# Block transposes on VectorE and SBUF-to-SBUF DMA in place of TensorE transposes, in a fused attention and feed-forward kernel

## The chip, the cores and the metric

The kernel runs on one core of one Trainium2 chip. A core has five engines with a queue each: TensorE (PE in the profile, with its weight loads as PEld), VectorE (DVE), ScalarE (ACT), GpSimd (POOL) and SyncE (SP, which here only issues DMA transfers), and 16 DMA engines that they share. The metric is the device time of one execution in microseconds; lower is better.

## The reference, cut to what matters

```python
xn = layernorm(x)                                  # x: 1 x 2048 x 640
qkv = xn @ wqkv                                    # 640 x 1920; 32 heads of 20
# position s attends to s, s-2, ..., s-14 (8 positions, 2 apart)
idx = pos[:, None] - 2 * arange(8)[None, :]
logits = einsum("bhsd,bhswd->bhsw", q, k[idx]) * 20 ** -0.5   # masked where idx < 0
o = einsum("bhsw,bhswd->bhsd", softmax(logits), v[idx])
s = o @ wo                                         # 640 x 640
g = silu(silu(xn @ w1) @ w2)                       # 640 x 1536, 1536 x 640
out = x + s * g
```

All inputs and the output are float32.

## The kernel before, in words

The 2048 positions are cut into four groups of 512: two halves of the sequence times even and odd positions, since the window of 8 steps by 2. In a group, a partition holds four positions (T = 4 tiles of 128), and attention works across the free dimension on VectorE.

Matrix products want the contracted dimension (640 = DC = 5 chunks of 128) on the partitions, so both the normalised x (`XIN`) and the attention output (`O`) must be turned from position-major to feature-major. TensorE reads fp32 data in a reduced form, so each operand is split into a high half (ScalarE's copy) and a low half (VectorE's difference), and each product is three matmuls: hi x hi, lo x hi, hi x lo. `TH` and `TL` hold the turned halves, two buffers each: one for the group's x, the other alternately for the previous group's turned o and the next group's turned x.

- `split_t` turns one chunk: four PE transposes into a `ROT` bank of PSUM (L429), ScalarE's high half (L433), VectorE's low half (L434).
- `qkv_phase(g)`: four quarters of eight heads (`CQ` = 160 columns); five weight chunks each, all four tiles (L633 to L635). ScalarE moves results to `KV` and `Q`; `halo` copies the neighbours' keys and values between partitions by DMA (L454); `scores` (L477, L480) and `values` (L509, L514, L517) are VectorE's attention. Between weight chunks, at the places in `O_AT`, `o_chunk` turns a chunk of the previous group's o.
- `wo_phase(g - 1)`: the previous group's output projection (L667, L669), its product with the gate `G` on VectorE (L699), the addition of x on POOL in `XR` (L706), and the store.
- `ffn_phase(g)`: twelve steps of w1 (L784 to L786), SiLU in two copies on ScalarE (L790, L791), the low half on VectorE (L792), w2 (L667, L669), and the gate's SiLU into `G` (L823). It loads and normalises the next group's x (L407, L419), and from step `XT_AT` = 7 on turns it a chunk per step. The last group turns its own o here, at `OL_AT`, and `wo_last` ends the kernel.
- The first group's x is turned by `first_quarter` (L558).

Weights come from DRAM once as float32 (`raw_load`, on SP), are split by ScalarE (L371) and VectorE or POOL (L374) into a slot of a ring of seven (`WR`), and are stored split to DRAM (L380, on SP); later uses fetch the split form through POOL's queue (L363). The ring runs seven weights ahead of PE.

The order on each engine is set before the kernel is built: `Weave.add` records every operation with the keys that it reads and writes, an estimated duration and a priority, and `Weave.order` plays them through a model of the engines (with `LANES` = 8 transfers in flight for a queue, `RATE` and `LAND` for a transfer). PE keeps the order of the program. Every other queue is emitted in the order of that model, so an instruction that has to wait on the chip holds back everything behind it in its queue. `lock` marks operations that the model keeps apart on VectorE and POOL.

Of the kernel before, what the change touches and what calls it, by code (L numbers as in the profile page):

```python
# [8 lines left out]
F32 = mybir.dt.float32  # L9
F32R = mybir.dt.float32r  # L10
AF = mybir.ActivationFunctionType
OP = mybir.AluOpType
# [19 lines left out]
WARM, WARM2 = 22, 3  # L32
HOLD = 3.4
LO = 10
X_AT = 2, 7, 8
TILE_AT = 1, 1.5, 5, 6
LOW_AT = 3
# [14 lines left out]


class Op:
    __slots__ = ("eng", "dur", "fn", "prio", "lock", "table", "nbytes", "seq", "left", "users", "ready", "start", "end")


class Weave:
# [16 lines left out]
        self.ops = []  # L75
        self.writer, self.readers = {}, {}

    def add(self, eng, dur, fn, reads=(), writes=(), prio=0.0, lock=False, table=None, nbytes=0):
        o = Op()
        o.eng, o.dur, o.fn, o.prio, o.lock, o.table, o.nbytes = eng, dur, fn, prio, lock, table, nbytes  # L80
# [12 lines left out]
        for k in reads:  # L93
            self.readers.setdefault(k, []).append(o)
        before.discard(o)
        o.left = len(before)
        for b in before:
            b.users.append(o)
        self.ops.append(o)
        return o  # L100

    def order(self):
# [12 lines left out]
        while len(done) < len(self.ops):  # L115
# [56 lines left out]
def local_attention_silu_ffn(ctx: ExitStack, tc: tile.TileContext, x, wqkv, wo, w1, w2, out):  # L172
# [19 lines left out]
    def tiles(name, n, shape, dtype=F32):  # L192
        return [sb.tile(shape, dtype, name=f"{name}{i}") for i in range(n)]
# [8 lines left out]
    SH = [None, sb.tile([P, TOK], F32R, name="sh1")]  # L202
    SL = [None, sb.tile([P, TOK], F32R, name="sl1")]
    ST.append(sb.tile([P, 2, 6], F32, name="st1"))
    SH[0] = sb.tile([P, TOK], F32R, name="sh0")
    SL[0] = sb.tile([P, TOK], F32R, name="sl0")
    SD = sb.tile([P, 2, T], F32, name="sd")
    mask = sb.tile([P, T, W], F32, name="mask")
    M = tiles("m", 2, [P, T, HQ])
# [44 lines left out]
        add("PE", dur, fn, reads, writes)  # L254
        clock[0] += dur

    def dma(fn, reads, writes, nbytes, prio, dur=0.45):
        add("SP", dur, fn, reads, writes, prio, nbytes=nbytes)

    clock = [0.0]  # L260

# [52 lines left out]
    def raw_load(k):  # L314
# [17 lines left out]
        if u[0] == "q":  # L332
            _, q, c = u
            w = qcols(q)
            all3 = wqkv[c * P:(c + 1) * P, :].rearrange("p (s m) -> p s m", s=3)

            def go():
                nc.sync.dma_start(r[:, :w], all3[:, 0, q * BQ:q * BQ + w])
                nc.sync.dma_start(r[:, w:].rearrange("p (s m) -> p s m", s=2), all3[:, 1:, q * CQ:(q + 1) * CQ])
            dma(go, [], kr, n * P * 4, 1 + k if k < 2 * DC else clock[0] + 5, dur=0.9)  # L340
            return
        elif u[0] == "w1":
            src = w1.rearrange("(c p) f -> p c f", p=P)[:, :, u[1] * P:(u[1] + 1) * P]
            dst = r.rearrange("p (c f) -> p c f", c=DC)
        else:
            m = wo if u[0] == "wo" else w2
            src, dst = m[u[1] * P:(u[1] + 1) * P, :], r
        dma(lambda: nc.sync.dma_start(dst, src), [], kr, n * P * 4, 1 + k if k < 2 * DC else clock[0] + 5)

    def w_load():  # L350
# [8 lines left out]
        kh, kl = ("wh", s), ("wl", s)  # L359
        due = clock[0]  # L360
        if what[i] == "load":
            src = halves[u]
            add("POOL", 1.0, lambda: nc.gpsimd.dma_start(both, src), [("half", u)], [kh, kl], due + 10,  # L363
                nbytes=2 * n * P * 4)
            return
# [57 lines left out]
    def split_t(src, skeys, c, i):  # L423
# [3 lines left out]
        def turn():  # L427
# [6 lines left out]
        dve(TOK, lambda: nc.vector.tensor_tensor(out=lo, in0=ps, in1=hi.bitcast(F32), op=OP.subtract),  # L434
            [kp] + kh, kl, 0)


    def evac_qkv(g, q, t, ps, kp):
        kv, w = KV[q], qcols(q)
# [81 lines left out]
    def o_chunk(g, c, i):  # L521
        qs = range(c * P // CQ, ((c + 1) * P - 1) // CQ + 1)
        split_t(O, [("o", q, t) for q in qs for t in (0, 2)], c, i)
# [92 lines left out]
        return ps  # L616

    def qkv_phase(g, i, io):
        for q in range(NQ):
            if g == 0 and q == 0:  # L620
                ps = first_quarter(i)
            else:
                ps = [bank() for t in range(T)]
                for c in range(DC):
# [10 lines left out]
                            nc.tensor.matmul(o, hi, wl, start=False, stop=c == DC - 1)  # L635
# [18 lines left out]
    O_AT = {(1, 1): 0, (1, 4): 1, (2, 3): 2, (3, 1): 3, (3, 3): 4}  # L654
    OL_AT = {8: 0, 9: 1, 10: 2, 11: 3, 12: 4}
    XT_AT = 7

    def tm_banks():
        a = [bank() for t in range(T)]
# [207 lines left out]
```

## Time and profile before

| | |
|---|---|
| runs shown, median (lowest to highest) | 642.38 us (642.08 to 643.38), 3 runs |
| the profiled execution's own time | 642.85 us |
| its span in the trace | 641.1 us |
| TensorE, VectorE, ScalarE, POOL busy | 634.1, 538.5, 207.3, 116.7 us |
| moved by DMA | 162.44 MB, mean 253 GB/s |
| TensorE transposes of x and o past the first x (L429) | 140 |

Busy time of an engine is the time in which at least one of its instructions runs; for PE, whose matmuls overlap, it says little on its own. In rows of a group, the numbers behind the bar are busy us and the mean ns of one, then the idle time before them and what ended it. In rows of the timeline and the chain, the first number is the start in us and the second the duration in us.

### The profile page before, as it was taken

The page shows a single profiled execution, that of the slowest core. Times are in us where ns is not written, and L with a number is a line of the kernel's source. Part 1 is how long each engine was busy: PE and PEld are TensorE (multiplying, and loading weights), DVE is VectorE, ACT ScalarE, POOL GpSimd, SP SyncE. Part 2 cuts the span into 40 slices and gives each one's busy share as a digit, 9 for nine tenths or more (in the row PEclk, how much of TensorE's full clock was granted, in tenths as well). Part 3 has the DMA queues.
Part 4 walks back from the last instruction along what each step waited for, and adds up shares of the span by engine and source line. Part 5 has one row for each costly group of instructions (what it writes and reads, how often), then busy time and mean ns, then how long its engine had stood idle before and what let it go on. Part 6 is the DMA issues. An engine that isn't in the chain of part 4 may idle for free.

```text
span 641.1 us, 9080 instructions
## 1 busy us (share of the span) xinstructions
PE 634.1 (99%) x3497; PEld 571.7 (89%) x3497; DVE 538.5 (84%) x539; ACT 207.3 (32%) x401; POOL 116.7 (18%) x168
## 2 busy tenths in 40 slices
PE   8999999999999999999999999999999999999997
PEld 6889899998889989999888998999988999899997
DVE  6599999999999999999839999998306999999714
ACT  5446463443443122324332221324313212133130
POOL 4410000000100044111112134111111214311100
PEclk9999999999999999999999999999999999999999
DMA  8999999877979998657699988965569996976522
GB/s 251 348 294 314 304 407 384 341 233 229 300 245 301 312 314 282 214 170 225 186 240 241 316 226 286 299 183 170 177 204 260 233 325 185 373 229 203 166 83 82
DMA packets 65386, 162.44 MB, mean 253 GB/s; under 512 B 6992, under 2 KB 29104, under 8 KB 65344
## 3 DMA queue, kind: packets, MB, share of 16 engines
q0 software_dynamic: 20016, 82.58, 42.5%
q1 hardware_dynamic: 45328, 79.29, 38.9%
q8 instruction: 27, 0.44, 0.3%
q14 instruction: 15, 0.12, 0.1%
HBM read 109.55 MB, written 34.16 MB: 224 GB/s over the span
## 4 chain that ended last, share of the span: by engine, by line
PE 95%; DVE 2%; DMA 1%; SPq 0%; issue 0%; DVEq 0%
PE acc L667 22%; PE acc L669 15%; PE acc L633 10%; PE acc L634 10%; PE acc L635 10%; PE rot L786 8%; PE rot L784 8%; PE rot L785 8%; PE rot L429 2%; DMA xin<-in_A_x_dram 1%; PE acc L579 1%; DVE gate L699 0%; DVE pr L477 0%; DVE sl L792 0%; PE rot L756 0%
## 5 line engine op out<-in xcount | busy, mean ns | idle before, releaser
L667 PE MATMUL acc<-w,sh 128*128 128x384 f32 x384 | 114.8, 337 | 0.0
L633 PE MATMUL acc<-w,th 128*128 128x512 f32 (+1 forms) x300 | 114.0, 380 | 0.0
L634 PE MATMUL acc<-w,tl 128*128 128x512 f32 (+1 forms) x300 | 112.7, 376 | 0.0
L635 PE MATMUL acc<-w,th 128*128 128x512 f32 (+1 forms) x300 | 112.5, 375 | 0.0
L669 PE MATMUL acc<-w,sh 128*128 128x256 f32 x384 | 107.2, 279 | 0.0
L477 DVE TENSOR_TENSOR pr<-q,kv 128x2560 f32<-128x2560 f32 x32 | 90.4, 2825 | 9.8 <-DMA kv<-kv 9.4
L784 PE MATMUL rot<-th,w 128*128 128x512 f32 x240 | 94.9, 395 | 0.0
L786 PE MATMUL rot<-th,w 128*128 128x512 f32 x240 | 93.7, 391 | 0.0
L785 PE MATMUL rot<-tl,w 128*128 128x512 f32 x240 | 93.7, 390 | 0.0
L509 DVE TENSOR_TENSOR pr<-e,kv 128x2560 f32<-128x2560 f32 x32 | 91.5, 2860 | 0.8
L480 DVE TENSOR_REDUCE l<-pr 128x128 f32<-128x2560 f32 x32 | 89.9, 2811 | 0.2
L790 ACT ACTIVATE sh<-rot 128x512 fp32r<-128x512 f32 x48 | 28.7, 599 | 150.9 <-PE rot L786 150.7
L514 DVE TENSOR_TENSOR pr<-pr 128x1280 f32<-128x1280 f32 x64 | 76.4, 1194 | 1.1
L669 PEld LDWEIGHTS acc<-w,sh 128*128 128x128 f32 x384 | 72.2, 188 | 1.5
L667 PEld LDWEIGHTS acc<-w,sh 128*128 128x128 f32 x384 | 72.1, 188 | 1.6
L363 POOL DMA_DIRECT2D w<-half_q x52 | 27.6, 531 | 247.5 <-DVE pr L514 92.7
L363 POOL DMA_DIRECT2D w<-half_w x72 | 38.4, 534 | 175.1 <-PE acc L669 72.8
L635 PEld LDWEIGHTS acc<-w,th 128*128 128x128 f32 x300 | 56.3, 188 | 8.9
L633 PEld LDWEIGHTS acc<-w,th 128*128 128x128 f32 x300 | 56.3, 188 | 8.6
L634 PEld LDWEIGHTS acc<-w,tl 128*128 128x128 f32 x300 | 56.4, 188 | 8.3
L667 PE MATMUL acc<-w,sl 128*128 128x384 f32 x192 | 58.7, 337 | 0.2 <-DVE sl L792 0.2
L434 DVE TENSOR_TENSOR tl<-rot,th 128x512 fp32r<-128x512 f32 x35 | 24.0, 685 | 35.5 <-ACT th L433 35.4
(88 smaller groups left out, 1006.0 us busy)
## 6 DMA issues: line engine op xcount, KB each, us to landing
w<-half_w POOLq DMA_DIRECT2D x72, 640.0 KB, 6.1
w<-half_q POOLq DMA_DIRECT2D x39, 512.0 KB, 3.9
half_w<-w SPq DMA_DIRECT2D x24, 640.0 KB
w<-half_wo POOLq DMA_DIRECT2D x15, 640.0 KB, 5.3
kv<-kv SPq DMA_DIRECT2D x16, 560.0 KB
half_q<-w SPq DMA_DIRECT2D x15, 512.0 KB
kv<-kv SPq DMA_DIRECT2D x16, 420.0 KB
gate<-in_B_w_dram SPq DMA_DIRECT2D x16, 320.0 KB
```

Source lines behind the costliest of these rows:

```text
L477: dve(2560, lambda t=t: nc.vector.tensor_tensor(out=PR, in0=win(qq[:, t:t + 2, :], W, 0), in1=win(kv[:, 0, t:t + 2, :], W, CQ), op=OP.mult ...
L480: dve(2560, lambda t=t: nc.vector.tensor_reduce(out=l[:, t:t + 2].rearrange("p t w h -> p (t w h)"), in_=PR.rearrange("p t w (h d) -> p (t ...
L509: dve(2560, lambda t=t, v=v: nc.vector.tensor_tensor(out=PR.rearrange("p t w (h d) -> p t (w h) d", d=DH), in0=e[:, t:t + 2].rearrange("p ...
L514: dve(2 * n * CQ, lambda n=n: nc.vector.tensor_tensor(out=PR[:, :, 0:n, :], in0=PR[:, :, 0:n, :], in1=PR[:, :, n:2 * n, :], op=OP.add), [] ...
L633: nc.tensor.matmul(o, hi, wh, start=c == 0, stop=False)
L634: nc.tensor.matmul(o, lo, wh, start=False, stop=False)
L635: nc.tensor.matmul(o, hi, wl, start=False, stop=c == DC - 1)
L667: nc.tensor.matmul(a[t][0][:, :CA], st, w[:, :CA], start=first, stop=last)
L669: nc.tensor.matmul(b[t // 2][0][:, h * CB:(h + 1) * CB], st, w[:, CA:], start=first and h == 0, stop=last, skip_group_check=True)
L784: nc.tensor.matmul(h, wh[:, cs], TH[i][:, c, :], start=c == 0, stop=False)
L785: nc.tensor.matmul(h, wh[:, cs], TL[i][:, c, :], start=False, stop=False)
L786: nc.tensor.matmul(h, wl[:, cs], TH[i][:, c, :], start=False, stop=c == DC - 1)
```

## The change

x of groups 1 to 3 and o of groups 0 to 2 are no longer turned by TensorE. VectorE transposes blocks of 32 x 32 within each quarter of 32 partitions, and DMA transfers between SBUF partitions put the blocks in the quarter where they belong; `split_sb` then makes the two halves from SBUF. The last group's o is still turned by `split_t` in `ffn_phase`.

- `turn_x` (in step 0 of `ffn_phase`): four VectorE transposes of 128 x 640 from `XIN` into a staging buffer (`KV[0]` for the first call, `G` for the others), 16 SP transfers of 32 x 640 elements (80 KB) back into `XIN`, then `split_sb`.
- `turn_o` (listed at the start of `qkv_phase`, once for each quarter): one VectorE transpose of 128 x 640 from `O` into `XR`, four SP transfers of 80 KB into `XIN`, which has to be free of turned x; `split_sb` follows when all four quarters have landed.
- In this form the 32 rows of a chunk in a partition quarter belong to one attention quarter, so the first load of each wo chunk gathers rows in that order with four transfers. The last group's wo, which is wanted in the plain order, is fetched with four POOL transfers for a chunk in place of one.
- In the planner these transfers get 3 us more of landing time (`late`).

```diff
+TURN = 3.0
+B = 32
+NB = P // B
+RUN = DC * TOK // NB
...
-                o.end = dma + self.LAND + (self.EARLY[1] if lanes[e][-1] and t < self.EARLY[0] else 0.0)
+                o.end = dma + self.LAND + o.late + (self.EARLY[1] if lanes[e][-1] and t < self.EARLY[0] else 0.0)
...
+        elif u[0] == "wo":
+            src = wo.rearrange("(q c a) m -> c q a m", q=NB, c=DC)[u[1]]
+
+            def by_quarter():
+                for q in range(NB):
+                    nc.sync.dma_start(r[q * B:(q + 1) * B], src[q])
+            dma(by_quarter, [], kr, n * P * 4, clock[0] + 5, dur=1.8)
+            return
...
+            if i >= len(units) - DC:
+                def by_block():
+                    for k in range(NB):
+                        q, c = divmod(NB * u[1] + k, DC)
+                        nc.gpsimd.dma_start(both[k * B:(k + 1) * B], halves["wo", c][q * B:(q + 1) * B])
+                add("POOL", 2.5, by_block, [("half", ("wo", c)) for c in range(DC)], [kh, kl], due + 10,
+                    nbytes=2 * n * P * 4)
+                return
...
+    XT = XIN.rearrange("p t d -> p (t d)")
+
+    def split_sb(keys, i):
+        v = XT.rearrange("p (i c t b) -> p c t i b", i=NB, c=DC, t=T)
+        xk = [("xin", t) for t in range(T)]
+        for c in range(DC):
+            kh, kl = t_keys(i, [c], kinds=["th"]), t_keys(i, [c], kinds=["tl"])
+            hi, lo = (w[i][:, c, :].rearrange("p (t i b) -> p t i b", t=T, i=NB) for w in (TH, TL))
+            act(TOK, lambda c=c, hi=hi: nc.scalar.activation(hi, v[:, c], AF.Copy), keys + xk, kh, 0)
+            dve(TOK, lambda c=c, hi=hi, lo=lo: nc.vector.tensor_tensor(
+                out=lo, in0=v[:, c], in1=hi.bitcast(F32), op=OP.subtract), keys + xk + kh, kl, 0, lock=True)
+
+    def turn_x(g, i):
+        if g == 0:
+            s1, ks = KV[0].rearrange("p s n m -> p (s n m)")[:, :T * D], halo_keys(0)
+        else:
+            s1, ks = G.rearrange("p t d -> p (t d)"), [("g", t, c) for t in range(T) for c in (0, CA)]
+        v = s1.rearrange("p (j c t b) -> p j c t b", j=NB, c=DC, t=T)
+        for t in range(T):
+            dve(D, lambda t=t: nc.vector.transpose(
+                out=v[:, :, :, t, :], in_=XIN[:, t, :].rearrange("p (c j a) -> p j c a", c=DC, j=NB)),
+                [("xin", t)], ks, 2)
+        for k in range(NB):
+            for j in range(NB):
+                dma(lambda k=k, j=j: nc.sync.dma_start(
+                    XT[j * B:(j + 1) * B, k * RUN:(k + 1) * RUN], s1[k * B:(k + 1) * B, j * RUN:(j + 1) * RUN]),
+                    ks, [("xt", k, j)], B * RUN * 4, clock[0], late=TURN)
+        split_sb([("xt", k, j) for k in range(NB) for j in range(NB)], i)
+        wv.writer["turned"] = wv.ops[-1]
+
+    def turn_o(q):
+        s = XR[q % 2]
+        dve(D, lambda: nc.vector.transpose(
+            out=s.rearrange("p (j t b) -> p t j b", j=DC, t=T),
+            in_=O[:, :, q * CQ:(q + 1) * CQ].rearrange("p t (j a) -> p t j a", a=B)),
+            [("o", q, t) for t in (0, 2)], [("xr", q % 2)], 2)
+        for k in range(NB):
+            dma(lambda k=k: nc.sync.dma_start(
+                XT[q * B:(q + 1) * B, k * RUN:(k + 1) * RUN], s[k * B:(k + 1) * B]),
+                [("xr", q % 2), "turned"], [("ot", q, k)], B * RUN * 4, clock[0], late=TURN)
...
     def qkv_phase(g, i, io):
+        if g:
+            for q in range(NQ):
+                turn_o(q)
+            split_sb([("ot", q, k) for q in range(NQ) for k in range(NB)], io)
...
-                    if g and (q, c) in O_AT:
-                        o_chunk(g - 1, O_AT[q, c], io)
...
-            if nxt is not None and XT_AT <= f < XT_AT + DC:
-                split_t(XIN, [("xin", t) for t in range(T)], f - XT_AT, ix)
+                turn_x(g, ix)
```

(The `SH` and `SL` tiles are also allocated in another order, in the same number and size.)

More of the change, by code (lines that the diff above doesn't have):

```diff
@@ L54 @@
 class Op:
-    __slots__ = ("eng", "dur", "fn", "prio", "lock", "table", "nbytes", "seq", "left", "users", "ready", "start", "end")
+    __slots__ = ("eng", "dur", "fn", "prio", "lock", "table", "nbytes", "late", "seq", "left", "users", "ready", "start", "end")
 class Weave:
@@ L76, in __init__, with add @@
         self.writer, self.readers = {}, {}
-    def add(self, eng, dur, fn, reads=(), writes=(), prio=0.0, lock=False, table=None, nbytes=0):
+    def add(self, eng, dur, fn, reads=(), writes=(), prio=0.0, lock=False, table=None, nbytes=0, late=0.0):
         o = Op()
+        o.late = late
         o.eng, o.dur, o.fn, o.prio, o.lock, o.table, o.nbytes = eng, dur, fn, prio, lock, table, nbytes
@@ L201, in local_attention_silu_ffn @@
     WR = tiles("w", RING, [P, 2 * D], F32R)
-    SH = [None, sb.tile([P, TOK], F32R, name="sh1")]
-    SL = [None, sb.tile([P, TOK], F32R, name="sl1")]
     ST.append(sb.tile([P, 2, 6], F32, name="st1"))
-    SH[0] = sb.tile([P, TOK], F32R, name="sh0")
-    SL[0] = sb.tile([P, TOK], F32R, name="sl0")
+    SH = tiles("sh", 2, [P, TOK], F32R)
+    SL = tiles("sl", 2, [P, TOK], F32R)
     SD = sb.tile([P, 2, T], F32, name="sd")
@@ L255, in pe, with dma @@
         clock[0] += dur
-    def dma(fn, reads, writes, nbytes, prio, dur=0.45):
-        add("SP", dur, fn, reads, writes, prio, nbytes=nbytes)
+    def dma(fn, reads, writes, nbytes, prio, dur=0.45, late=0.0):
+        add("SP", dur, fn, reads, writes, prio, nbytes=nbytes, late=late)
     clock = [0.0]
@@ L344, in raw_load @@
             dst = r.rearrange("p (c f) -> p c f", c=DC)
[L345 to L347 removed]
+        elif u[0] == "wo":
[5 more added lines that the diff above has]
+            return
+        else:
+            src, dst = w2[u[1] * P:(u[1] + 1) * P, :], r
         dma(lambda: nc.sync.dma_start(dst, src), [], kr, n * P * 4, 1 + k if k < 2 * DC else clock[0] + 5)
```

2 lines of the change are left out of this document (removed).

## The prediction

> **What bounds the kernel now.** I read the page's busy shares first, then the waits of TensorE, then the chain that ended last.
>
> ```profile
> span 641.1 us, 9080 instructions
> ...
> PE 634.1 (99%) x3497; PEld 571.7 (89%) x3497; DVE 538.5 (84%) x539; ACT 207.3 (32%) x401; POOL 116.7 (18%) x168
> ...
> DVE  6599999999999999999839999998306999999714
> ...
> PE 95%; DVE 2%; DMA 1%; SPq 0%; issue 0%; DVEq 0%
> ```
>
> ```profile
> PE rot L532 <- POOL ident masks.py:199: 1.4, 1, 1.4
> PE acc L579 <- ACT w L371: 1.1, 2, 0.6
> PE acc L667 <- DVE sl L792: 0.2, 1, 0.2
> ```
>
> TensorE (PE) waits for another engine 2.7 us in all, 2.5 of them at the start, and the chain lies on it for 95% of the span: whatever leaves the PE queue and brings no wait shortens the kernel one for one. VectorE (DVE) comes second. Its digits are 9 from about 32 us to 304 us and then leave two gaps (slices 19 and 20, and 27 to 30): work added early is paid from a full engine, work added later from these gaps.
>
> What the transposes cost PE has to be read from the chain, since PE's durations overlap:
>
> ```profile
> by line: PE acc L667 22.0%; PE acc L669 14.6%; PE acc L633 10.0%; PE acc L634 10.0%; PE acc L635 10.0%; PE rot L786 8.2%; PE rot L784 8.2%; PE rot L785 8.2%; PE rot L429 2.4%; DMA xin<-in_A_x_dram 1.4%; PE acc L579 1.3%; DVE gate L699 0.5%;
> ...
> 108.59 0.44 PE rot L429 x4
> ...
> 513.96 0.44 PE rot L429 x4
> ```
>
> These are the first and the last of 30 groups of four transposes: five chunks of x for each of groups 1 to 3 and five of o for each of groups 0 to 2. (Five more, for the last group's o, make up the 2.4%: 35 x 0.44 = 15.4 us of 641.1.) All 30 lie on the chain at 0.44 us each.
>
> **The change, part by part.**
>
> *Removed from PE:* 30 x 0.44 = 13.2 us. The group of operations gives another figure:
>
> ```profile
> L429 PE MATMUL rot<-ident,o 128*128 128x128 f32 x80 | 12.0, 272 | 0.0
> ```
>
> By 272 ns each, 120 transposes would be 32.6 us. But four of them take 0.44 us of chain, 0.11 each, because the next starts before the last one's modelled end; I take 0.44. The Trainium skill (TensorE: Matmul & The Clock Gate, Part 4: PE-mode transpose) gives about 275 ns for a transpose inside a kernel, which agrees with the 272 as a duration; used as a price it would make the saving 33 us.
>
> *Added to DVE:* four block transposes per x and four per o, 24 of 128x640. None is in the trace, so I bound one: from below by the cheapest 128x640 pass, 0.55 us (four LayerNorm passes in 2.19), from above by a pass over four times the elements, 2.81. The nearest row is an ordinary 128x640 pass, 0.82 us, which I take:
>
> ```profile
> L480 DVE TENSOR_REDUCE l<-pr 128x128 f32<-128x2560 f32 x32 | 89.9, 2811 | 0.2
> ...
> L374 DVE TENSOR_TENSOR w<-raw,w 128x640 fp32r<-128x640 f32 x13 | 10.7, 820 | 1.5 <-ACT w L371 1.5
> ...
> 149.48 0.88 DVE L407 BATCH_NORM_STATS2 st<-xin 128x6 f32<-128x320 f32 x2
> ...
> 157.03 2.19 DVE L419 TENSOR_SCALAR xin<-xin,mv,sd 128x640 f32<-128x640 f32 x4
> ```
>
> That is 24 x 0.82 = 19.7 us (13 to 67), DVE at 558 us (552 to 606) of some 630. It costs nothing while its results come before PE asks for them; dates follow. The Trainium skill (VectorE: DVE Perf Modes, Rules for kernel authors) speaks against the change: for a full 128x128 transpose use TensorE where a PSUM result will do. Its table of transpose paths has 311 ns for 128x128 in 32x32 blocks, so by that page 120 x 0.311 = an estimated 37 us on DVE; the trace shows no such instruction.
>
> *Splits:* the high halves (ACT) and low halves (DVE) stay, 30 each, but read SBUF rather than PSUM.
>
> ```profile
> L434 DVE TENSOR_TENSOR tl<-rot,th x35: 678/684/692, 109.7 to 616.7; 128x512 fp32r<-128x512 f32 x35
> L792 DVE TENSOR_TENSOR sl<-sf,sh x48: 679/685/4421, 70.2 to 612.8; 128x512 fp32r<-128x512 f32 x48
> ```
>
> L792 is the same operation with both inputs in SBUF: median 685 against 684 ns, so I add nothing; its 4.42 us maximum (beside GpSimd's additions L706) says that a low half can now be caught once in a while, up to 3.7 us, hidden except next to a date.
>
> *DMA:* 16 transfers of 80 KB per x and per o, 96 in all, 7.9 MB beside 162 (5%); 3 more for each first load of a wo chunk (15 on SP) and for each of the last group's wo loads (15 on POOL). An issue is 0.33 us or more on SP and 0.53 on POOL. PE does not see these unless something queued behind comes late.
>
> *Moved:* x of the next group now shares its buffer with turned x and turned o, so its load and LayerNorm wait until o's split. LayerNorm for group 2, 6.4 us of DVE (from 149.48 on: 4.1 of statistics, 0.2, 2.19), moves from before the end of group 0's attention to after it. That pays for most of the new DVE work there.
>
> **Dates.** Where can PE catch up with the longer path?
>
> ```profile
> 184.61 0.49 DVE L517 TENSOR_TENSOR o<-pr 128x320 f32<-128x320 f32 x1
> ...
> 202.39 0.34 PE L667 MATMUL acc<-w,th 128*128 128x384 f32 x1
> ...
> 325.85 0.69 DVE L434 TENSOR_TENSOR tl<-rot,th 128x512 fp32r<-128x512 f32 x1 [6.63 <-ACT th L433]
> ...
> 482.98 0.69 DVE L434 TENSOR_TENSOR tl<-rot,th 128x512 fp32r<-128x512 f32 x1 [24.97 <-ACT th L433]
> ```
>
> Group 0: its attention ends at 185.1. With seven transposes ahead (5.7), and 6.4 moved away, it ends near 184.5. Then one transpose (0.8), four issues (about 1.6), a landing (two wo loads below took 6.0 and 6.9 us for 320 KB each; these are 80 KB, so 5.5), and the first chunk's ACT and DVE halves (0.6 + 0.7, behind a DVE pass of up to 2.8): ready at 194 to 197. All chunks need all quarters now, so no chunk can go earlier. The output projection (202.39 before) asks at 202.4 - 10 x 0.44 = 198.0. One to four us to spare: the tightest of the three. If the cover goes, PE waits out the difference.
>
> Group 1's attention ended 6.6 us before the L434 that ran at 325.85, at 319.2, and its projection starts near 349 (halfway between 202.39 and the 513.96 of the chain's last o row, less 20 x 0.44); group 2's ended by 458 (DVE idle 24.97 us before 482.98), against 501 (513.96 less 13.2). These have 15 us and more, even with some 8 us of transposes and splits behind them. Turned x has most of an FFN phase (80 us) in each group.
>
> The weights near that first projection are tight too:
>
> ```profile
> 182.00 0.36 SPq L348 DMA_DIRECT2D raw<-in_A_wo_dram  x1
> ...
> 188.02 0.74 ACT L371 ACTIVATE w<-raw 128x640 fp32r<-128x640 f32 x1 [5.09 <-DMA raw<-in_A_wo_dram]
> ...
> 201.60 0.33 SPq L348 DMA_DIRECT2D raw<-in_A_wo_dram  x1
> ...
> 208.47 0.74 ACT L371 ACTIVATE w<-raw 128x640 fp32r<-128x640 f32 x1 [4.40 <-DMA raw<-in_A_wo_dram]
> ...
> 224.56 0.53 POOL L363 DMA_DIRECT2D w<-half_w  x1 [10.41 <-DMA half_wo<-w]
> ...
> 237.62 0.39 PE L784 MATMUL rot<-th,w 128*128 128x512 f32 x1
> ```
>
> ```profile
> w<-half_w POOLq DMA_DIRECT2D x72, 640.0 KB, 6.1
> ...
> w<-half_wo POOLq DMA_DIRECT2D x15, 640.0 KB, 5.3
> ```
>
> The fifth wo chunk, split from 208.5 to 210.1, is used four chunks of 3.55 us after 202.4, at 216.6: 6.5 us ahead. PE comes 4.4 us earlier, and each load takes three more issues (1 us) behind o's DMAs on SP, whose last four wait for DVE while the key halos and wo loads queue behind them. The FFN weight that POOL could only fetch at 224.56 (its ring slot was still being stored) lands some 6.1 us later, near 231, for use at 237.62, which becomes 233.2: 2 us to spare, if nothing ahead of it moves. As all three margins hold by these figures, I take 0.2 us of wait at each, what the one wait of PE for DVE inside the kernel costs now: 0.6. The bounds are 0 (PE has no more than that 0.2 us of inner waits to win back) and, if the landings' spread (0.9), a caught low half (3.7) and one more DVE pass (2.8) all fall on these dates, 7.4.
>
> The tail keeps PE's transposes and both sides shift alike:
>
> ```profile
> 606.96 0.48 DVE L517 TENSOR_TENSOR o<-pr 128x320 f32<-128x320 f32 x1
> ...
> 611.46 0.60 PE L429 MATMUL rot<-ident,o 128*128 128x128 f32 x4
> ...
> 611.92 0.53 POOL L363 DMA_DIRECT2D w<-half_wo  x1 [2.88 <-PE rot L786]
> ...
> 619.42 0.34 PE L667 MATMUL acc<-w,th 128*128 128x384 f32 x1
> ```
>
> Attention's last o is 4 us ahead of its transpose; group 2's o work leaves that stretch of DVE, so this does not shrink. The last wo chunk, now four fetches (1.6 us more), had 7.5 us from its issue to the projection's start: enough for 1.6 + 5.3.
>
> **The sum.** The profiled execution took 642.85 us (span 641.1 and 1.75 around it); 642.85 - 13.2 + 0.6 = 630.25. The median of the runs shown, 642.38, is 0.47 below it: 629.8.
>
> **Rivals.**
> *The first projection is late* (chance 0.17). The three margins around 198 to 233 us are missed by 3 to 7.4 us together, because SP stands behind o's last quarter. Time: 629.2 without waits, plus those, 632 to 637. For it: margins of 1 to 4 us built on landings of 5 to 7 us. Against it: PE's earlier arrival also frees ring slots and finishes key evacuations earlier, and SP's queue follows them.
> *DVE becomes the bound: slower* (0.07). One mechanism: the block transposes are long. Eight of them lie ahead of group 0's projection, on an engine with no gap there; each 1 us above 0.82 makes o 8 us later, and about 3 us are spare. The 13.2 us are eaten at 8 x (p - 0.82) = 16.2, p = 2.85 us; from there the kernel is slower, at 4 us per transpose by 25 - 3 - 13 = 9 us, 652. For it: no row shows the instruction. Against: an ordinary pass of the same size is 0.82.
> *The full duration counts* (0.02). If a transpose holds PE for 272 ns, 642.4 - 32.6 = 610. The 0.44 us of the chain speak against it.
> *The gain is hidden* (0.04): new waits of PE, of 0.44 us at the places where the transposes sat, give the time back: 641.5 to 643. Against it: PE waits nowhere in those phases now.
> The forecast has 0.70, with a range of its own of 628.6 to 633.
>
> **Numbers.** Within 0.2% (1.3 us, about what a measurement can tell here): 0.04, the hidden gain. Slower: 0.07. Faster: 0.70 + 0.17 + 0.02 = 0.89. The range takes the forecast's own and the late projection: 628 to 637.
>
> **What would show it.** L429's groups fall from 35 to 5 on the chain (2.4% to about 0.35%). A new DVE transpose row has 24 instructions near 0.82 us. PE's waits stay below 4 us, and the new ones name L667's low or high half or a weight near 198 us. The prediction is wrong if a transpose costs above 2 us, if the DVE's low halves wait long for the turned pieces, or if PE waits for tl, th or w at the first projection by more than 3 us.

## The result: 2.5% slower, and the profile after

| | before | after |
|---|---|---|
| runs beside each other, median (lowest to highest) | 642.88 us (642.08 to 643.65) | 659.19 us (656.43 to 660.31) |
| ratio, 95% interval | | 1.0247 (1.021 to 1.0285) |
| profiled execution, span | 642.85, 641.1 us | 660.1, 658.1 us |

Ratios leave out executions more than 1.5% slower than the fastest of their kernel; medians and ranges do not, but for one of 1658 us (e14).

The forecast of 629.8 us, its range and its sign were wrong. These are the lines of the page after that answer to those of before (span, busy shares, digits of TensorE and of its clock, chain):

```profile
span 658.1 us, 9073 instructions
...
PE 629.8 (96%) x3377; PEld 564.1 (86%) x3377; DVE 555.9 (84%) x563; ACT 207.2 (31%) x403; POOL 122.1 (19%) x183
...
PE   8999999989998399999999999999999998999997
...
PEclk9999999999999689999999999999999999999999
...
PE 65%; DVE 17%; DMA 11%; SPq 3%; issue 2%; ACT 1%; DVEq 0%; ACTq 0%
```

TensorE no longer carries the chain: 65% where it was 95%. Its waits (total, times, longest):

```profile
PE acc L729 <- ACT w L389: 12.1, 2, 9.8
PE acc L729 <- DVE sl L853: 6.3, 3, 3.1
PE acc L729 <- DVE w L392: 1.7, 3, 1.0
...
PE acc L699 <- ACT gate L884: 1.1, 1, 1.1
PE acc L699 <- ACT q L505: 0.5, 1, 0.5
```

With the start all waits are 23.8 us, against 2.7 before: 21.1 more. The hole in slice 13 (counted from 0: 214 to 230 us) is the first output projection, 12.1 + 1.7 us for the second to the fifth output weight, 9.8 of them for the fourth (L389 is ScalarE's split, L371 before; L392 the low half). The 6.3 us are low halves of SiLU that VectorE makes late, at 142 to 145, 402 and 556 us; at the first and the last of these places they stand behind a pass of attention of 2.8 to 2.9 us (142.53 and 553.50) in VectorE's own queue.

TensorE's busy time fell by 4.3 us only, not by 13.2. The rows say why. Windows of the changed kernel (busy us and instructions of PE, PEld, DVE, ACT and POOL, then granted clock, DMA share, GB/s):

```profile
143.00:146.00 3.00, 0.20 (x3) 0.00 (x1) 3.00 (x3) 0.00 (x0) 0.53 (x1) 1.00 0.85 232
146.10:149.70 3.60, 3.60 (x15) 3.60 (x16) 3.60 (x3) 1.47 (x3) 0.00 (x0) 0.53 0.47 119
214.20:218.10 3.90, 3.90 (x18) 3.85 (x16) 3.86 (x3) 0.00 (x0) 0.00 (x0) 0.56 1.07 374
221.10:235.10 14.00, 5.98 (x21) 5.58 (x22) 13.60 (x20) 3.06 (x4) 1.06 (x2) 0.51 0.92 281
559.00:562.80 3.80, 3.80 (x13) 3.24 (x12) 3.77 (x2) 0.00 (x0) 0.90 (x2) 0.55 0.98 264
...
235.00:245.00 10.00, 10.00 (x56) 8.94 (x55) 7.12 (x10) 1.09 (x2) 4.68 (x5) 1.00 0.91 304
```

and a pair of its matmuls with the start of the next, in the third stretch at a low clock and behind it, from the timeline:

```profile
232.85 0.52 PE L729 MATMUL acc<-w,th 128*128 128x384 f32 x1
233.17 0.41 PE L731 MATMUL acc<-w,th 128*128 128x256 f32 x1
233.38 0.52 PE L729 MATMUL acc<-w,th 128*128 128x384 f32 x1
...
235.54 0.34 PE L729 MATMUL acc<-w,th 128*128 128x384 f32 x1
235.72 0.28 PE L731 MATMUL acc<-w,th 128*128 128x256 f32 x1
235.84 0.34 PE L729 MATMUL acc<-w,th 128*128 128x384 f32 x1
```

After each of the longer waits the granted clock is about a half for some microseconds; a pair then takes 0.53 us (232.85 to 233.38) instead of 0.30 (235.54 to 235.84). PE busy, 629.8, against 634.1 - 13.2 = 620.9, puts the half clock at 8.9 us. Sum: -13.2 + 21.1 + 8.9 = +16.8; the span grew by 17.0. As the 8.9 is a difference, this sum has to close; the clock is its check. The four stretches above at 0.51 to 0.56 hold 17.3 us of busy time, and busy time times the missing share of the clock is 8.0 us there. The Trainium skill (TensorE: Matmul & The Clock Gate, HAM oscillation) says to leave no idle gap of TensorE above some 3.4 us, or the clock falls to half; the trace agrees after the 9.8 us wait, and shows it after a 2.8 us one as well. The same wait need not cost the same: after one of 2.35 us at 114 us, the clock from 116 to 120 us was 0.61 in e10 and 1.00 in e2 (both below).

Why were the weights late? SyncE's queue in the changed kernel ahead of and in the first output projection:

```profile
185.82 5.39 SPq L353 DMA_DIRECT2D raw<-in_A_wo_dram  x4
191.30 3.17 SPq L496 DMA_DIRECT2D xin<-xr  x4
...
197.47 4.05 SPq L353 DMA_DIRECT2D raw<-in_A_wo_dram  x4
...
204.03 2.88 SPq L353 DMA_DIRECT2D raw<-in_A_wo_dram  x4
...
210.85 0.90 SPq L418 DMA_DIRECT2D xin<-in_A_x_dram  x2
211.84 3.16 SPq L516 DMA_DIRECT2D kv<-kv  x4
215.11 11.82 SPq L353 DMA_DIRECT2D raw<-in_A_wo_dram  x8
```

Before, the five loads left at 182.00, 183.87, 195.66, 197.03 and 201.60. Now the second stands behind turned o, and the fourth and fifth stand behind 1.3 MB of the next x and four halo transfers. Most of the 11.8 us of their eight pieces is no issuing. Three leave by 216.8, the fourth at 220.85, and SyncE's waits from 210 to 228 us say why:

```profile
SPq L353 <- DMA kv<-kv: 4.1, 2, 2.8
SPq L353 <- DMA xin<-in_A_x_dram: 4.1, 1, 4.1
```

For 8.2 us a piece could not leave before x and halos ahead of it had landed. The fourth piece is the eighth transfer behind the second half of x, for which it waits, so a limit of eight in flight, as in the planner's model, fits. Cutting a load in four thus costs twice: by its issues, and because later pieces come under this limit. Rows by source line (durations min/median/max in ns) price an issue and a block transpose, the first in the kernel before, the others in the changed one:

```profile
L454 SPq DMA_DIRECT2D kv<-kv x64: 607/872/2055, 27.5 to 519.2; - x64
...
L482 SPq DMA_DIRECT2D xin<-kv x16: 588/590/1751, 88.2 to 100.4; - x16
L496 SPq DMA_DIRECT2D xin<-xr x48: 507/590/1002, 111.5 to 489.1; - x48
...
L477 DVE STREAM_TRANSPOSE kv<-xin x4: 802/822/846, 84.5 to 87.4; 128x640 f32<-128x640 f32 x4
L491 DVE STREAM_TRANSPOSE xr<-o x12: 801/845/847, 95.9 to 486.4; 128x640 f32<-128x640 f32 x12
```

The transposes cost what was taken (0.82); an issue costs 0.59 us, not 0.33. The kernel before had a nearer row than the loads from DRAM that gave 0.33: its halo transfers, between SBUF partitions too, at 0.87. ScalarE, which splits the weights, keeps an order too (its timeline):

```profile
211.64 0.74 ACT L389 ACTIVATE w<-raw 128x640 fp32r<-128x640 f32 x1 [7.42 <-DMA raw<-in_A_wo_dram]
...
224.28 0.30 ACT L431 ACTIVATE sd<-mv,epst 128x4 f32<-128x4 f32 x1 [10.61 <-DVE mv L427]
227.36 0.74 ACT L389 ACTIVATE w<-raw 128x640 fp32r<-128x640 f32 x1 [2.79 <-DMA raw<-in_A_wo_dram]
```

The square root of the moved LayerNorm stands ahead of the last two splits, but the split behind it still waited 2.79 us for its data.

### The profile page after: what moved, and what is told of

Read it like the earlier page. It is cut to its first block, busy times and chain, and to the rows that moved or that the text cites. A ratio compares the mean times of both kernels' runs of the same rounds, so it can differ in the third digit from the quotient of the medians.

```text
span 658.1 us, 9073 instructions
## 1 busy us (share of the span) xinstructions
PE 629.8 (96%) x3377; PEld 564.1 (86%) x3377; DVE 555.9 (84%) x563; ACT 207.2 (31%) x403; POOL 122.1 (19%) x183
## 4 chain that ended last, share of the span: by engine, by line
PE 65%; DVE 17%; DMA 11%; SPq 3%; issue 2%; ACT 1%; DVEq 0%; ACTq 0%
PE acc L729 17%; PE acc L731 11%; PE rot L846 8%; PE rot L847 8%; PE rot L845 8%; PE acc L701 4%; PE acc L700 4%; PE acc L699 4%; DMA kv<-kv 4%; DVE pr L539 3%; DVE l L542 3%; DMA xin<-in_A_x_dram 3%; DVE pr L571 3%; DVE pr L576 2%; SPq L516 1%
## 5 line engine op out<-in xcount | busy, mean ns | idle before, releaser
L539 DVE TENSOR_TENSOR pr<-q,kv 128x2560 f32<-128x2560 f32 x32 | 90.2, 2820 | 14.2 <-DMA kv<-kv 13.8
L729 PE MATMUL acc<-w,th 128*128 128x384 f32 x160 | 51.9, 355 | 13.8 <-ACT w L389 12.1
```

What stands on the lines that cost most here:

```text
L539: dve(2560, lambda t=t: nc.vector.tensor_tensor(out=PR, in0=win(qq[:, t:t + 2, :], W, 0), in1=win(kv[:, 0, t:t + 2, :], W, CQ), op=OP.mult ...
L729: nc.tensor.matmul(a[t][0][:, :CA], st, w[:, :CA], start=first, stop=last)
```

## The experiments

Four theories. Q: SyncE's in-order queue (number and place of its transfers) brings late what is needed at a fixed time (Q1 and Q2 in the expectations: by the place, by the number). A: ScalarE's in-order queue is held by the moved LayerNorm. V: VectorE's added time sets the end. B: the added bytes do. Times are medians, with the ratio to the kernel before measured beside them. The variants' own runs scatter by up to 2.6%, those of the kernel before by some 0.4%; so a single profile of a variant tells the place of a wait rather than its size.

### What costs: VectorE, the bytes or the issues?

**Merged transfers (e4).** The same transposes and bytes, but 24 transfers of 128 partitions for 96 of 32:

```diff
-        for k in range(NB):
-            for j in range(NB):
-                dma(... XT[j*B:(j+1)*B, k*RUN:(k+1)*RUN], s1[k*B:(k+1)*B, j*RUN:(j+1)*RUN] ...)
+        for k in range(NB):
+            dma(... XT[:, k*RUN:(k+1)*RUN], s1[:, k*RUN:(k+1)*RUN] ...)      # o: one for each quarter
```

> The whole change, but the turned pieces go in 24 transfers of 128 partitions (320 KB) in place of 96 of 32 partitions (80 KB): the same bytes and waits, a quarter of the issues; blocks stay in their partition quarter, so x and o are turned only within quarters and the products are of misplaced features. wo still comes in quarters. Theory Q: SP reaches the wo loads earlier, PE's waits at the first projection at least halve: 643 to 652 us. Theories V and B: unchanged, 657 to 661 us.

641.99 us, ratio 0.9999 (0.9978 to 1.002). TensorE's longest waits:

```profile
PE acc L725 <- DVE sl L849: 5.7, 4, 3.5
...
PE acc L695 <- ACT q L501: 1.4, 1, 1.4
```

and SyncE's rows for x of group 1 and for the fourth and fifth output weight:

```profile
87.56 2.50 SPq L481 DMA_DIRECT2D xin<-kv  x4
...
194.74 4.13 SPq L353 DMA_DIRECT2D raw<-in_A_wo_dram  x8
```

No weight is waited for any more. 17 us go without one byte or transpose less: V and B are not the cause of these. The eight pieces now leave in 4.1 us, with no wait for a landing. But this variant is still 12 us above the forecast: its waits are 8.8 us more than before (5.7 of them low halves on VectorE), and its busy time, 624.8, is 3.9 above 620.9. For the low halves VectorE's queue is a cause that no run took away by itself.

**Every block transpose twice (e7).**

```diff
-        for t in range(T):
+        for t in [t for t in range(T) for n in range(2)]:      # and turn_o's one in a loop of two
```

> The changed kernel with each of the 24 VectorE block transposes done twice (the second writes the same bytes): 24 x 0.82 = 19.7 us more of VectorE, nothing else. Theory V (VectorE's time sets the end): slower by 10 to 20 us, 669 to 679. Theories Q and A: only four of them lie ahead of a date that is missed (o of group 0, 3.3 us), the others have slack: slower by 0 to 5 us, 659 to 664.

655.25 us (649.28 to 661.07), ratio 1.017 (1.0119 to 1.0221): below every expectation, and not slower than the changed kernel, with VectorE at 574.3 us where it had 555.9. That speaks against V again. The planner also ordered the queues anew, with the output weights' loads ahead of x, so the small gain may belong to the order.

**All 96 transfers issued from POOL (e5).**

```diff
-                dma(lambda ...: nc.sync.dma_start(XT[...], s1[...]), ks, [("xt", k, j)], ...)
+                add("POOL", 1.0, lambda ...: nc.gpsimd.dma_start(XT[...], s1[...]), ks, [("xt", k, j)], ...)
```

> The whole change, but all 96 transfers of turned pieces are issued from POOL's queue, which has no weight to fetch before 127 us; wo's quartered first loads stay on SP. Same bytes, same transposes. Theory Q: SP's queue is as free as before but for 15 issues: PE's wait at the first projection under 5 us, 634 to 645 us, unless the weights that POOL fetches come late behind pieces that wait for VectorE. Theories V and B: unchanged, 655 to 661 us.

643.31 us, ratio 1.0017 (0.9993 to 1.0041). One wait of 7.8 us is left at the first output projection, for the fifth weight, whose load still stood behind x. The Trainium skill (DMA: Bandwidth & Descriptors, Issuing engines are not separate DMA queues) says of issuing from several engines that it will "only save the time on the sequencer it takes to initiate the DMA, which is usually small relative to the DMA itself"; here, with the reordering that came with it, that moved 16 us. How much of it is issue time and how much waiting for landings, no run separates.

**Output weights loaded in one transfer each (e1):**

```diff
-                for q in range(NB):
-                    nc.sync.dma_start(r[q * B:(q + 1) * B], src[q])
+            dma(lambda: nc.sync.dma_start(r, wo[c*P:(c+1)*P, :]), ...)
```

> The whole change, but the first load of each wo chunk is one SP transfer again in place of four (15 fewer issues, same bytes); the rows then come in plain order, so the projection of groups 0 to 2 multiplies o with misplaced rows of wo. Theory Q (SP's queue: in-order issues, a limited number in flight, so the wo loads of the first projection come late): PE's waits at the first projection fall from 13.8 us to under 5, and the stretch at a lower granted clock behind them goes: 645 to 650 us. Theory V (VectorE's 24 block transposes and its later results are the cost) and theory B (the added bytes on the DMA engines): unchanged, 657 to 661 us.

652.65 us, ratio 1.0164 (1.0134 to 1.0193): the quarters cost some 6.5 us. That misses theory Q's 645 to 650, and TensorE still waits 11.2 us there. The last two loads now leave together at 209.4 us; theory A's row stands in front of their splits, but these then wait 2.38 us more for data:

```profile
221.61 0.30 ACT L424 ACTIVATE sd<-mv,epst 128x4 f32<-128x4 f32 x1 [13.29 <-DVE mv L420]
224.29 1.55 ACT L382 ACTIVATE w<-raw 128x640 fp32r<-128x640 f32 x2 [2.38 <-DMA raw<-in_A_wo_dram]
```

They left behind x (203.54) and the halos (206.07), and took 14 to 15 us to land; before, the fifth left ahead of the halos and landed in 6.9.

### Which part costs?

**x only (e2), and x of group 1 only (e10):**

```diff
-            for q in range(NQ):
-                turn_o(q)
+                    if g and (q, c) in O_AT:
+                        o_chunk(g - 1, O_AT[q, c], io)      # output weights in plain order, both kernels
-                turn_x(g, ix)
+                if g == 0:                                  # the second kernel only
+                    turn_x(g, ix)                           # x of groups 2 and 3 by split_t
```

> Only x of groups 1 to 3 is turned by VectorE and DMA (12 transposes, 48 transfers); o is turned by TensorE and wo is loaded as before. Removed from PE: 15 x 0.44 = 6.6 us. Theory Q: nothing is put in front of the wo loads and no o waits for landing, PE's waits at the first projection stay under 2 us: 637 to 643 us. Theory V (loss in proportion to the transposes): half of the loss of 16 us, about 651 us.

> Only x of group 1 is turned the new way (4 transposes, 16 transfers); everything else as before. 2.2 us off PE. Theory Q1: PE waits 5 us or more for weights in the first two groups: 646 to 652 us, slower than before. Rival A and theory V: nothing stands in ScalarE's way and four transposes are 3.3 us on VectorE: 640 to 642 us.

648.8 us (1.0099, 1.008 to 1.0118) and 652.73 us (1.0162, 1.0136 to 1.0188). The first missed theory Q's 637 to 643. Four transposes and 16 transfers alone cost 10.4 us. SyncE's and ScalarE's timelines of the second, and its longest waits of TensorE:

```profile
85.86 13.79 SPq L467 DMA_DIRECT2D xin<-kv  x16
...
185.94 0.41 SPq L351 DMA_DIRECT2D raw<-in_A_wo_dram  x1
198.94 1.26 SPq L351 DMA_DIRECT2D raw<-in_A_wo_dram  x1
...
210.77 0.36 SPq L351 DMA_DIRECT2D raw<-in_A_wo_dram  x1
...
224.44 0.74 ACT L374 ACTIVATE w<-raw 128x640 fp32r<-128x640 f32 x1 [10.37 <-DMA raw<-in_A_wo_dram]
```

```profile
PE acc L713 <- ACT w L374: 4.7, 1, 4.7
PE acc L713 <- DVE w L377: 2.3, 1, 2.3
```

SyncE is held for 13.8 us in the middle of the first loads of weights, which go through few raw buffers one behind the other. The stream never makes this up: of its last members, the output weights, the first two leave at 185.94 and 198.94 instead of 182.00 and 183.87, the fifth at 210.77 instead of 201.60. The fifth now leaves behind the last halos (206.67; before, they left at 203.05, behind it) and is split 13.7 us later, not 6.9. TensorE pays 2.3 us at 114 us, and 4.7 at the fifth output weight, over 100 us after the hold. Adding x of groups 2 and 3 on top gains 3.9 us (652.7 to 648.8).

**o only (e3), and all but x of group 1 (e9):**

```diff
-                turn_x(g, ix)
+            if nxt is not None and 7 <= f < 7 + DC:         # second kernel: if g == 0 and ..., turn_x for the others
+                split_t(XIN, [("xin", t) for t in range(T)], f - 7, ix)
```

> Only o of groups 0 to 2 is turned by VectorE and DMA (12 transposes, 48 transfers, wo in quarters); x is turned by TensorE. Removed from PE: 6.6 us. Theory Q: o's transfers and the quartered wo loads are all still on SP ahead of the first projection, so PE waits there for 8 us or more: 648 to 660 us. Theory V: half of the loss, about 651 us, and no more wait at the first projection than elsewhere.

> The whole change, but x of group 1 is turned by TensorE as before (25 chunks new, 11.0 us off PE). Theory Q1: x of group 1 is the harmful part, its 16 transfers hold SP for 12.7 us at 88 to 101 us, where the first loads and stores of the weights go through SP, and the whole chain of fresh weights reaches the first projection late; without them PE's wait there falls under 4 us: 633 to 643 us. Rival A: ScalarE is held by the square root of group 2's LayerNorm (10.6 us before 224.28), which the shared buffer puts in front of the last two wo splits; this stays as it is, PE's wait at the first projection stays at 9 us or more: 650 to 660 us.

659.49 us (650.0 to 660.73; 1.0187, 1.0108 to 1.0266) and 651.68 us (1.0141, 1.0125 to 1.0157). By its ratio, o with its quartered weights cannot be told from the whole. Leaving x of group 1 out gives back 7.5 of the 17 us, and the wait for the output weights falls from 13.8 to 6.3; theory Q1 had expected under 4, and 633 to 643 us.

**Only the parts with slack, o of groups 1 and 2 and x of groups 2 and 3 (e6):**

```diff
-        if g:
+        if g > 1:
             for q in range(NQ):
                 turn_o(q)                                   # o of group 0 by o_chunk, x of group 1 by split_t
-            if i >= len(units) - DC:
+            if u[0] == "wo" and i < len(units) - DC:        # stored plain, fetched in four by POOL for groups 1 and 2
```

> x of group 1 and o of group 0 by TensorE as before; x of groups 2 and 3 and o of groups 1 and 2 the new way; wo stored in plain order and fetched by quarters in groups 2 and 3 (four POOL transfers for a chunk). 20 x 0.44 = 8.8 us off PE. Theory Q (the loss sits where fresh weights go through SP, in the first two groups): waits of PE under 5 us in all, 634 to 640 us, faster than before. If the loss is in every group alike (theory V, or key halos and SiLU low halves that come late behind the turned transfers): two thirds of it stay, 646 to 654 us.

647.54 us (642.69 to 653.21; 1.0057, 1.0025 to 1.009), not the 634 to 640 of theory Q: no first load of a weight is late, but at the second output projection ScalarE holds evacuations behind the same square root (theory A):

```profile
363.88 0.30 ACT L424 ACTIVATE sd<-mv,epst 128x4 f32<-128x4 f32 x1 [14.41 <-DVE mv L420]
```

### What holds the output weights?

**The square root held back (e13)** until the first SiLU of the phase:

```diff
+            if nxt is not None and f == (1 if g else 0):
+                ln_rstd(0, T, held=[("sh", 0)] if g else [])
```

> The changed kernel with one edit of order: the square root of LayerNorm (ScalarE) of groups 2 and 3, and what follows from it, may start only after the first SiLU of the feed-forward phase, so it no longer stands on ScalarE ahead of the last two splits of the output weights and of the evacuations. All transposes and transfers stay. Theory A (ScalarE's queue is held by the square root, which waits for a LayerNorm that now comes late): the wait at the first output projection falls from 12.1 by at least 5 us, with some half-clock time behind it: 646 to 652. Theory Q (SyncE's many issues bring the raw weights late): the last two raw loads still leave SP at 215 us and the wait stays near 10 us: 656 to 660. Theory V (VectorE is the bound): no change, 659.

658.53 us (1.0247, 1.0205 to 1.0289): no gain. TensorE waits as long in one piece, and with the square root gone ScalarE waits for the data itself:

```profile
PE acc L729 <- ACT w L389: 13.1, 1, 13.1
```

```profile
227.41 0.74 ACT L389 ACTIVATE w<-raw 128x640 fp32r<-128x640 f32 x1 [16.70 <-DMA raw<-in_A_wo_dram]
```

At this place A was only the visible releaser; the loads were late behind it.

**x's load behind the output weights (e16)**, and the same with POOL's issues (e17):

```diff
-    dma(... rows(xg, g)[:, t:t + n]), [], [("xin", u) ...])
+    dma(... rows(xg, g)[:, t:t + n]), [("rawwo", c) for c in range(DC)], [("xin", u) ...])
+    dma(by_quarter, [], kr + [("rawwo", u[1])], ...)
```

> The changed kernel with one edit: the load of group 2's x, which the change puts on SyncE between the third and the fourth load of the output weights, is put behind the fifth. The block transposes, the 96 transfers, their queue and the order on TensorE stay. Theory Q1 (the 1.3 MB of x in front of the last two loads of the output weights, on one queue, makes these late: held up 11.8 us in the changed kernel, 5.4 us where they went first): the wait of 12.1 us at the first output projection falls below 5 us, with its half-clock time, and the kernel comes to 645 to 652. Theory Q2 (the number of small transfers alone makes the queue late, x or not): the wait stays at 8 us or more, 655 to 660. Theory A (ScalarE held by the square root): the square root moves behind too, so A expects 645 to 652 as well; holding the square root alone has already left the wait at 13.1.

> The edit of the run before together with all 96 turned transfers issued from POOL. With POOL's issues alone TensorE still waited 7.8 us at the first output projection, where the fifth output weight's load stood behind x (643.3 us). Theory Q1: this wait goes, with some 2 to 4 us of half clock: 631 to 637, which beats the kernel before by the transposes taken from TensorE. Theory Q2: the wait stays, 640 to 645.

656.95 us (1.0212, 1.0177 to 1.0247): the wait for the output weights falls from 13.8 (12.1 + 1.7 in the changed kernel) to 9.5 us, short of what was expected; the eight pieces still take 8.7 us to leave, 4.7 of them waits for halos and other transfers ahead to land. With POOL's issues the wait falls from 8.4 to 4.3, but the kernel takes 658.7 us (1.0264, 1.0211 to 1.0316): other queues came out in another order, with waits for evacuations (6.9) and for SiLU (2.6). That miss was not resolved further.

**The planner's prices raised (e18)** (issue 0.8 for 0.45, a quartered load 4.0 for 1.8 and 3 us more of landing), no work changed:

```diff
-                    ks, [("xt", k, j)], B * RUN * 4, clock[0], late=TURN)
+                    ks, [("xt", k, j)], B * RUN * 4, clock[0], dur=0.8, late=TURN)      # turn_o too
-            dma(by_quarter, [], kr, n * P * 4, clock[0] + 5, dur=1.8)
+            dma(by_quarter, [], kr, n * P * 4, clock[0] + 5, dur=4.0, late=TURN)
```

> The changed kernel with the planner's estimates alone altered: 0.8 us in place of 0.45 for the issue of a turned transfer, 4.0 in place of 1.8 and 3 us of landing more for a load of an output weight in four. The instructions are the same; their order on SyncE, ScalarE and VectorE changes, so that the first loads of the output weights stand ahead of the last quarter's halo transfers. Theory M (the order was planned with issues priced too low): the wait of 12.1 us at the first output projection falls by 5 us or more, 644 to 653. Theory Q2 (the queue has too many small transfers, whatever their order): the wait stays or another takes its place, 655 to 661.

652.88 us (1.0166, 1.0135 to 1.0197), the wait at the projection 8.0: some 6 us of the loss come from an order planned with issues that were too cheap.

**Turned x through DRAM (e19)**, 15 issues for 48 and 3.9 MB more:

```diff
+        kept = dram.tile([P, T * D], F32, name=f"turned{g}")
+        back = kept.rearrange("(k p) (j r) -> j p k r", k=NB, j=NB)
+        dma(lambda: nc.sync.dma_start(kept, s1), ...)
+        for j in range(NB):
+            dma(lambda j=j: nc.sync.dma_start(XT[j * B:(j + 1) * B].rearrange("p (k r) -> p k r", k=NB), back[j]), ...)
```

> The changed kernel with turned x sent through DRAM: one store of 1.3 MB and four loads of 320 KB in place of 16 transfers of 80 KB, so 15 issues on SyncE in place of 48, and 3.9 MB more moved. Theory Q2 (the number of issues): the 12.7 us in which SyncE was held by x of group 1 go, and with them most of what x of group 1 alone had cost (10.4 us): 646 to 653. Theory B (bytes moved): no gain, 659 to 662.

654.42 us (650.34 to 663.3; 1.0168, 1.0092 to 1.0243): better at more bytes, which speaks against B. Two of the four runs took 650.4 us, inside theory Q's range, the others 658.4 and 663.3; the quartered weights are still waited for.

### Versions meant to beat both

**Three combinations** of the edits above (e14, e15, e20):

```diff
 # 1: the changed kernel
+ turned transfers from POOL; square root held; x's load behind the output weights
 # 2: only the parts with slack
+ turned transfers from POOL; square root held
 # 3: o of group 0 by TensorE, output weights stored plain
+ all turned x through DRAM
```

> The changed kernel with all 96 turned transfers issued from POOL, the square root held as in the run before, and x of the next group loaded only after the five loads of the output weights. The VectorE transposes and the bytes are those of the changed kernel. Theories Q and A together: both the late weights and the held ScalarE queue go, PE waits fall to some 2 to 6 us and the saving of 13.2 shows: 631 to 638. Theory V: as with POOL's issues alone, 641 to 645.

> x of group 1 and o of group 0 are turned by TensorE, the rest by VectorE; the turned transfers are issued from POOL and the square root is held. Saving left on PE: 20 of 30 groups, 8.8 us. Theories Q and A: 633.5 plus 1 to 5 us of waits, 634 to 639. Theory V, or any price of the transposes themselves: 642 or more.

> All x turned by VectorE and through DRAM as in the run before; o of group 0 by TensorE, so the output weights are loaded in one transfer each, and later fetched by blocks; o of groups 1 and 2 as in the changed kernel. 25 of 30 groups leave TensorE, 11 us. SyncE has 47 issues for turned data in place of 96 and 15 fewer for weights. Theory Q2: 637 to 645, near the kernel before or better. Theory A (ScalarE's queue held by the moved LayerNorm) adds waits of some 5 to 10 us around the second output projection: 643 to 650.

654.8 to 661.6 us (1.023, 1.0174 to 1.0287), 650.93 us (1.0112, 1.0053 to 1.017) and 647.52 us (1.0057, 1.0029 to 1.0085). The first two missed; the third came out where theory A had it, the square root again in front of the evacuations (13.1 us). Each kept some o, and with it an x that must wait for `XIN`.

**Only x of groups 2 and 3, issued from POOL (e21):**

```diff
+                if g > 0:
+                    turn_x(g, ix)          # transfers by nc.gpsimd; no turn_o, plain output weights
+            if g == 0 and 7 <= f < 7 + DC:
+                split_t(XIN, ..., f - 7, ix)
```

> Only x of groups 2 and 3 is turned the new way, its 32 transfers issued from POOL; x of group 1 and all o by TensorE, the output weights loaded in one transfer each in plain order. XIN is not shared with o, so x's load and its LayerNorm stay where they were. 10 of 30 groups leave TensorE, 4.4 us. If the harm comes from work that the new path puts in front of dated work in the queues (theories Q2 and A), none of it is left here but POOL's 32 issues: 637.5 to 641. If turned data by VectorE and DMA costs time of its own wherever it stands (VectorE's time, bytes): 642 or more.

638.02 us (637.85 to 638.74), ratio 0.9932 (0.9918 to 0.9946): faster than both kernels, than the one before by 4.4 us, which is 10 x 0.44. All its waits of TensorE:

```profile
PE rot L579 <- POOL ident masks.py:199: 1.4, 1, 1.4
PE acc L626 <- ACT w L374: 0.7, 1, 0.7
PE acc L713 <- DVE sl L842: 0.5, 1, 0.5
```

and the first of its two turned x in the timeline:

```profile
243.51 3.02 DVE L462 STREAM_TRANSPOSE gate<-xin 128x640 f32<-128x640 f32 x4
248.13 2.96 POOL L467 DMA_DIRECT2D xin<-gate  x6
```

They come after the last first load of a weight, and some 50 us before TensorE asks for this x (302 us).

## Why the prediction was wrong, by its steps

- *30 x 0.44 us leave TensorE*: held. Ten groups alone gave 4.4 us (e21). The chain's price was right, and the 272 ns of duration were not the price.
- *Added to VectorE*: held at 0.80 to 0.85 us, some 20 us for all 24 (the estimate of 37 us beside it was too high), and the splits at 0.685; the rival "VectorE becomes the bound" fell with e4 and e7.
- *DMA: "an issue is 0.33 us or more on SP", "PE does not see these unless something queued behind comes late"*: this step failed. The price was 0.59, 96 x 0.59 = 57 us of SyncE, and what follows waited for landings besides (8.2 us among the pieces of the last two output weights); and what is queued behind was asked only at o's dates. The row for x of group 1 was dismissed because turned x had an FFN phase of slack; yet the 16 transfers stand in front of the first loads of weights, which have none (e10: 10.4 us).
- *Moved: "That pays for most of the new DVE work there"*: failed. The move was entered as VectorE's relief only. Its 1.3 MB load came to stand in front of two output weights (e16: about 4 us of the wait), and its square root in front of ScalarE's evacuations (e6).
- *Dates, group 0*: o's first chunk was split at 199.7 us, not at 194 to 197, 1.7 us after the date of 198.0. That cost nothing, as TensorE, held up at 143 us, came at 201.83. It waited for the weights, 13.8 us. Of their margin of 6.5 us, 4.4 had been taken for TensorE's earlier arrival and 1 for extra issues; but the fifth stands behind the extra issues of all five, 15 x 0.33 = 5 us by the prediction's own price, so this margin did not hold by its own figures.
- *Bound of the waits, 7.4 us*: built from spreads of single landings; a queue in order adds up. It missed also the low halves of SiLU elsewhere (6.3 us), and it priced a wait at its length: the half clock behind it added 8.0 to 8.9 us.
- The rival "the first projection is late" named the right place, with SyncE's queue as cause, but its price (632 to 637 us) was the bound's, and it looked for the hold at o's last quarter alone.

What stays open: the shares of the causes at the first projection do not add up (quarters 6.5, x of group 1 7.5, x's load about 4, the planner's prices 6, of one loss of 17), since they overlap and each reordering makes waits elsewhere. No run measured the half clock by itself, and it comes and goes: e2 and e10 have the same two waits of 2.3 and 4.7 us, but mean clocks of 0.997 and 0.992 over the span. The runs of one variant differ with it too: of e4's, 640.13 us had 0.997 and 647.31 us 0.992.

## What to carry to other kernels

Before moving work to an idle engine, list for each of its DMA issues what stands behind it in the queue, and give that a date, also where the moved result itself has slack; a stream of loads through few buffers, with its last member due at a fixed time, has none. In kernels with in-order queues move first what lies after such a stream (here x of two groups: the full 0.44 us a group), and leave the rest. Price a TensorE wait of some microseconds at more than its length: here 21.1 us of waits came with some 8 us of work lost to the clock.

## What was not expected of the hardware

An issue on SyncE of a transfer between 32 SBUF partitions took 0.59 us at the median and up to 1.75, against 0.36 for a load of an output weight from DRAM before. In a busy queue eight pieces of 80 KB took 11.8 us to leave, 8.2 of them waits for transfers ahead to land. TensorE's granted clock was 0.53 right after a wait of 2.8 us; after one of 2.35 us it was 0.61 in one variant and 1.00 in another.
